# Bulk loads cut into row pieces and issued a few per step from SyncE, with six layer-norm tiles transposed on TensorE

## The chip, the cores and the metric

The kernel runs on one core of a Trainium2 chip. The metric is device time in microseconds (us), as the median of several executions. A kernel's executions mostly lie within 1 to 2% of each other; the comparisons below give a ratio with a 95% interval.

Names used throughout: TensorE (PE, with its weight loads as PEld), VectorE (DVE), ScalarE (ACT), GpSimd (POOL) and SyncE (SP) are the engines; "SPq" and the like are their instruction queues where DMAs are issued. A DMA issued by SyncE goes to the queue q1 of the profile, one by ScalarE to q10, one by GpSimd to q0.

## The reference

Four layers, alternating a linear-attention block A and a sliding-window block B (window 256), forward and then all gradients. B = 1, S = 2048, D = 640, 32 heads of 20, bf16. Both B layers share weights, and so do both A layers.

```python
x = x + A(layernorm(x), A_wqkv, A_wo)     # layer 0: phi(q) (phi(k)^T v) / normalizer, then @ wo
x = x + B(layernorm(x), B_wqkv, B_wo)     # layer 1: softmax over the last 256 keys, then @ wo
x = x + A(layernorm(x), A_wqkv, A_wo)     # layer 2
x = x + B(layernorm(x), B_wqkv, B_wo)     # layer 3
# returned: x and the gradients for A_x, A_wqkv, A_wo, B_wqkv, B_wo, given grad_out
```

## The kernel before

The stages in order of time, as they are named below:

| stage | from ... to | what runs |
|---|---|---|
| start | begin ... first QKV matmul | loads of x and of the weights |
| first | ... first mixing matmul | layer 0: layer norm and QKV of 16 tiles |
| fwd | ... first score matmul of the backward attention | rest of the forward pass |
| gap3 | ... first `acc` product | pipeline of layer 3's attention fills; weights are transposed |
| att3 | ... first dense matmul | backward attention of layer 3, 8 groups of heads x 16 blocks |
| dns3 | ... first weight-gradient matmul | dense backward of layers 3 and 2, up to the start of the next attention |
| att1 | ... last `acc` product | backward attention of layer 1, filled with weight-gradient matmuls of layers 3 and 2 |
| dns1 | ... last dense matmul | dense backward of layers 1 and 0 |
| last | ... end | weight gradients of layers 1 and 0 |

In the attention every unit computes scores, `e` (ACT), `ds` (DVE), and turns `ds` into `dsT`. One half of `dsT` is turned on TensorE, the other half by a DMA transpose that SyncE issues. Five steps later the products `acc` read it. Bulk loads come from three engines:

```python
def dma(self, out, in_, eng=None, piece=None):
    eng = eng or self.nc.scalar                      # ScalarE unless said otherwise
    kw = dict(max_dma_last_dim=piece) if piece else {}
    ...
def tr(self, out, in_):
    self.nc.sync.dma_start_transpose(out=out, in_=in_)      # always SyncE
# ... load_w:
    elif name == "WT":                               # 2400 KB, GpSimd
        self.dma(t, self.WT_d[:, kind], self.nc.gpsimd, piece=D)
# ... flip_w: transposed weights, three buffers in turn
        t = pool.tile([P, n, P], BF, name=f"wt{n}")
        self.tr(t, w[k * P:(k + 1) * P, :])
        if late is not None:
            self.dma(*late, self.nc.gpsimd)          # the store that frees the buffer: GpSimd
# ... seg_first:
    for c in range(0, self.TT, 2):
        self.dma(self.car[:, c:c + 2, :], xv[:, c:c + 2, :])     # x, ScalarE, W after the first
# ... seg_attention_bwd:
    def load(g):                                     # the slabs of a group of heads
        r = slabs[g] = slab_B if g % 2 else self.slab_A
        for i, n in enumerate(("QT", "KT", "VT")):
            if g > 0:
                self.dma(r[n], sv["qkvT"][:, i * G + g, :])      # 512 KB each, ScalarE
        for t in range(0, T, 512 if g == 0 else T):
            ts = slice(t, t + (512 if g == 0 else T))
            self.dma(r["dOT"][:, ts], sv["dOT"][:, g, ts], nc.sync if g == 0 else None)
    def load_rows():                                 # 7.7 MB, GpSimd
        for t in range(0, TT, 4):
            self.dma(qk_r[:, t:t + 4, :], sv["qk"][:, t:t + 4, :], nc.gpsimd)
            self.dma(dO_r[:, t:t + 4, :], sv["dO"][:, t:t + 4, :], nc.gpsimd)
    # ... dscore(u, half, ps):
        if half == 0:
            self.tr(dsT_of[u][:, 0:2 * nkt, :], ds_of[u][:, 0:2 * nkt * P])
# ... wgrad: operands of 2560 and 1280 to 1920 KB, GpSimd
    self.dma(lhs, lhs_d, nc.gpsimd, piece=D)
    ...
    self.dma(r[:, :, 0:w], rhs_d[:, :, c * w:(c + 1) * w], nc.gpsimd)
```

The softmax here doesn't subtract the row's maximum and nothing guards it: scores larger than these inputs give would overflow.

Of the kernel before, what the change touches and what calls it, by code (L numbers as in the profile page):

```python
# [15 lines left out]
P = 128  # L16
# [6 lines left out]
class Kern:  # L23

    def __init__(self, ctx, tc, x0, A_wqkv, A_wo, B_wqkv, B_wo, grad_out, outs):
# [12 lines left out]
        assert D == 640 and T % 512 == 0  # L38
        self.c_att = float(DH) ** -0.5
        self.x0, self.grad_out = x0, grad_out  # L40
        self.out_x4, self.out_gx, self.out_dWA, self.out_dWoA, self.out_dWB, self.out_dWoB = outs
# [77 lines left out]

    def dma(self, out, in_, eng=None, piece=None):  # L120
        eng = eng or self.nc.scalar
        kw = dict(max_dma_last_dim=piece) if piece else {}
        with self.nc.allow_non_contiguous_dma(reason="strided layouts"):
            eng.dma_start(out=out, in_=in_, **kw)

# [13 lines left out]
    def load_w(self, pool, kind, name):  # L139

        D, DT = self.D, self.DT
        if name == "W":
            t = pool.tile([P, DT, self.QT], BF, name=f"W{kind}")
            self.dma(t, self.Wqkv[kind].rearrange("(kt p) n -> p kt n", p=P))
        elif name == "Wo":
            t = pool.tile([P, DT, D], BF, name=f"Wo{kind}")
            self.dma(t, self.Wo[kind].rearrange("(kt p) n -> p kt n", p=P))
        elif name == "WT":
            t = pool.tile([P, self.QTT, D], BF, name=f"WT{kind}")
            self.dma(t, self.WT_d[:, kind], self.nc.gpsimd, piece=D)  # L150
        else:
            t = pool.tile([P, DT, D], BF, name=f"WoT{kind}")
            self.dma(t, self.WoT_d[:, kind], self.nc.gpsimd, piece=D)
        return t

    def permute_w(self):

        w = 4 * DH
        out = self.Wp.rearrange("r (g t c) -> r t g c", t=3, c=w)
        in_ = self.Wqkv[1].rearrange("r (t g c) -> r t g c", t=3, c=w)  # L160
        for t in range(3):
            self.dma(out[:, t], in_[:, t], self.nc.sync)

# [21 lines left out]

    def ln(self, l, tt, pw):
        nc, D = self.nc, self.D
        x = self.car[:, tt, :]
        st = pw.tile([P, 2, nc.vector.BN_STATS_DIM], F32, name="ln_st")
        for c in range(2):  # L190
            nc.vector.bn_stats(st[:, c, :], x[:, c * self.HD:(c + 1) * self.HD])
        mv = pw.tile([P, nc.vector.BN_AGGR_DIM], F32, name="ln_mv")
        nc.vector.bn_aggr(mv, st)
        lv = pw.tile([P, 1], F32, name="ln_lv")
        nc.scalar.activation(lv, mv[:, 1:2], ACT.Ln, bias=self.eps_t, scale=1.0)
        rs = self.rs[l][:, tt:tt + 1]
        nc.scalar.activation(rs, lv, ACT.Exp, scale=-0.5)
        hn = pw.tile([P, D], BF, name="ln_hn")
        nc.vector.tensor_scalar(out=hn, in0=x, scalar1=mv[:, 0:1], scalar2=rs, op0=ALU.subtract, op1=ALU.mult)
        hnT = pw.tile([P, self.DT, P], BF, name="ln_hnT")  # L200
        self.tr(hnT, hn)
        self.dma(self.hn_d[l][:, tt, :], hn)
        return hnT
# [212 lines left out]
    def seg_first(self, acc, pf, pWA, pWB):  # L416

        with ExitStack() as st:
            pw = self.pool(st, "w0w", 3)
            pkv = self.pool(st, "w0kv", 6)  # L420
            pps = self.pool(st, "ps", 8, PSUM)
            xv = self.tm(self.x0)
            for c in range(0, self.TT, 2):
                self.dma(self.car[:, c:c + 2, :], xv[:, c:c + 2, :])
                if c == 0:
                    W = self.load_w(pWA, 0, "W")
            self.Wf = (W, self.load_w(pWB, 0, "Wo"), self.load_w(pf, 1, "Wo"), self.load_w(pWB, 1, "W"))
            tiles = []
            for tt in range(self.TT):
                hnT = self.ln(0, tt, pw)  # L430
                self.drain(self.A_qkv(0, tt, hnT, W, tiles, pw, pkv, pps))
                self.kv_step(tiles, acc, tt, pps)

    def seg_pair(self, l, mbd, acc, on_tail=None):

        nc, TT, H, G = self.nc, self.TT, self.H, self.G
        with ExitStack() as st:
# [78 lines left out]
            for u in range(-AHEAD, n + LAG):  # L516
                if on_tail is not None and u == n - G:
                    on_tail()
                if u + AHEAD < n:
                    evs[u + AHEAD] = self.B_scores(l + 1, *units[u + AHEAD], ring, pe, ps_s)  # L520
# [154 lines left out]
    def load_A(self, l):  # L675
        for i, n in enumerate(("QT", "KT", "VT")):
            self.dma(self.slab_A[n], self.sv[l]["qkvT"][:, i * self.G, :], self.nc.gpsimd)

    def seg_attention_bwd(self, l, fill, pace, side=None):
# [7 lines left out]
        with ExitStack() as st:  # L687
# [8 lines left out]
            def load(g):  # L696
                r = slabs[g] = slab_B if g % 2 else self.slab_A
                for i, n in enumerate(("QT", "KT", "VT")):
                    if g > 0:
                        self.dma(r[n], sv["qkvT"][:, i * G + g, :])  # L700
                for t in range(0, T, 512 if g == 0 else T):
                    ts = slice(t, t + (512 if g == 0 else T))
                    self.dma(r["dOT"][:, ts], sv["dOT"][:, g, ts], nc.sync if g == 0 else None)

# [3 lines left out]
            def load_rows():  # L708
                for t in range(0, TT, 4):
                    self.dma(qk_r[:, t:t + 4, :], sv["qk"][:, t:t + 4, :], nc.gpsimd)  # L710
                    self.dma(dO_r[:, t:t + 4, :], sv["dO"][:, t:t + 4, :], nc.gpsimd)

# [110 lines left out]

            load(0)
            load_rows()
            n = len(units)
            for s in range(n + JL):
                if side is not None:
                    next(side, None)
                if s < n and units[s][1] == 6 and units[s][0] + 1 < G:  # L830
                    load(units[s][0] + 1)
# [39 lines left out]
    def dense_weights(self, l, pool):  # L871
        w = [self.load_w(pool, 1, "WT"), self.load_w(pool, 0, "WoT"), pool.tile([P, 6, self.D], BF, name="mbdT")]
        self.dma(w[2], self.sv[l - 1]["mbdT"], self.nc.gpsimd, piece=self.D)
        return w

    def seg_dense_bwd(self, l, w, mid):

        nc, TT, D, DT, H, HD = self.nc, self.TT, self.D, self.DT, self.H, self.HD
        a = l - 1
        sv = self.sv[a]  # L880
        with ExitStack() as st:
            pb = self.pool(st, "bacc")
# [6 lines left out]
            with ExitStack() as s2:  # L889
# [69 lines left out]
                for s in range(-2, TT + 3):  # L959
                    for f, d in plan:  # L960
                        if 0 <= s + d < TT:
                            f(s + d)
                    if s == 3:
                        WTA = self.load_w(pb, 0, "WT")
                        WoTB = self.load_w(pb, 1, "WoT") if a > 0 else None
# [3 lines left out]
            with ExitStack() as s2:  # L969
# [59 lines left out]
                def flip_dO(t):  # L1029
                    ring, pos = self.dOT_ring[(t // 4) % 2], t % 4  # L1030
                    self.flip(self.do_slabs[t % 3], self.G, ring[:, :, pos * P:(pos + 1) * P], pt, [nc.scalar.copy])
                    if pos == 3:
# [4 lines left out]
                        *tail[2:])  # L1037
                for s in range(-4, TT + 2):
                    for f, d in plan:
                        if 0 <= s + d < TT:  # L1040
# [5 lines left out]

    def wgrad(self, l, pools, last, which=(0, 1), wait=0):

# [5 lines left out]
                (self.o_d[l], self.g_d[l], HD, self.part[kind][1], (self.out_dWoA, self.out_dWoB)[kind], False)]  # L1054
        jobs = [jobs[i] for i in which]
        for lhs_d, rhs_d, w, part, out, perm in jobs:
            lhs = pW.tile([P, TT, D], BF, name="wg_l", bufs=2 if last else 1)
            self.dma(lhs, lhs_d, nc.gpsimd, piece=D)
            n = part.shape[1] // w

            def load(c):
                r = pw.tile([P, TT, wq], BF, name="wg_r")
                self.dma(r[:, :, 0:w], rhs_d[:, :, c * w:(c + 1) * w], nc.gpsimd)
                return r
            rhs = load(0)
            for _ in range(wait):
                yield
            for c in range(n):
                nxt = None
                for m in range(DT):  # L1070
# [5 lines left out]
                    for tt in range(TT):  # L1076
                        nc.tensor.matmul(ps, lhsT=lhs[:, tt, rows], rhs=rhs[:, tt, 0:w],  # L1077
                                         start=(tt == 0), stop=(tt == TT - 1))
                        yield
                    if m == 0 and c + 1 < n:  # L1080
                        nxt = load(c + 1)
                    if last:
# [16 lines left out]
    def run(self):  # L1099
        self.permute_w()  # L1100
        s_att = self.ctx.enter_context(ExitStack())
        with ExitStack() as st:
# [12 lines left out]
            for l in (0, 2):  # L1115
                with ExitStack() as s2:
                    pm = self.pool(s2, "mbd")
                    mbd = self.close_A(l, acc, pm)
                    self.seg_pair(l, mbd, acc, None if l == 0 else tail)
                if l == 0:  # L1120
                    sA.close()
        for l in (3, 1):
            with ExitStack() as s2:
                s_wg, s_ps, w = ExitStack(), ExitStack(), []

                def fill():
                    pools = self.wg_pools(s_wg) + [self.pool(s_ps, "wgp", 1, PSUM)]
                    yield from self.wgrad(3, pools, False, (0, 1), 48)
                    yield from self.wgrad(2, pools, False, (0, 1), 48)
                    s_wg.close()  # L1130
# [15 lines left out]
                else:  # L1146
                    self.seg_attention_bwd(l, it, lambda s: 11.8)
                    self.drain(it)
# [3 lines left out]
                    def mid():  # L1152
# [4 lines left out]
                        def run():  # L1157
                            for k in (1, 0):
                                yield from self.wgrad(k, pools, True, wait=1)
                        last.extend((pools, run()))  # L1160
# [59 lines left out]
```

## Time and profile before

The median was 2788.51 us in the first three runs (2772.23 to 2792.51). The profiled execution has a span of 2800.1 us.

The page of the kernel before. The first line is busy time with its share of the span; then come 40 slices of 70 us each, in tenths: PE busy, the granted TensorE clock, and the busy share of the DMA engines.

```profile
PE 2235.1 (80%) x27724; PEld 1420.6 (51%) x27724; DVE 1360.2 (49%) x2554; ACT 1277.1 (46%) x2171; POOL 1076.5 (38%) x1433
...
PE   3879997489986146998889795897799878969979
...
PEclk9989998698795566787899797898899889979999
DMA  9588984498896998877784775688677669486585
```

TensorE is busy 80% of the time; the other engines are at half or less. It is the engine to keep fed. Weak places of the PE row that the change touches are the beginning and the slices from about 910 to 1120 us, the start of att3. The clock row is weak in the latter too.

The list of waits (engine, line and tile that waited, then what it waited for, total us, times, longest us):

```profile
PE acc L786 <- DMA dsT<-ds: 143.2, 17, 60.1
...
PE d L232 <- DMA ln_hnT<-ln_hn: 59.3, 7, 44.3
...
POOL WoT_d L124 <- DMA qk_r<-qk: 40.3, 2, 36.7
```

The products waited 143.2 us for DMA-transposed tiles, once for 60.1 us. The first QKV matmul waited 44.3 us for its transposed tile.

The DMA queues (packets, MB, share of 16 engines) and some issues (how often, KB each, median us from issue to landing):

```profile
q1 hardware_dynamic: 647888, 198.29, 41.8%
q10 hardware_dynamic: 110624, 142.25, 16.9%
q0 software_dynamic: 35152, 144.56, 16.8%
...
qk_r<-qk POOLq DMA_DIRECT2D x8, 1280.0 KB, 31.6
...
wg_l<-hn POOLq DMA_DIRECT2D x4, 2560.0 KB, 14.9
...
dsT<-ds SPq DMA_TRANSPOSE x256, 4.0
```

The bytes of the bulk loads are in q10 (ScalarE) and q0 (GpSimd); the `dsT` transposes are among the many small packets of q1 (SyncE). A `dsT` tile lands in 4.0 us at the median; the view of that tile gives 26.0 us as the longest.

The 60 us wait can be read from two timelines (start, duration, engine, line, tile; in brackets the idle time before it and what ended it). SyncE around 940 us:

```profile
940.64 57.44 SPq L127 DMA_TRANSPOSE wt<-in_A_wqkv_dram  x2
998.50 5.00 SPq L127 DMA_TRANSPOSE dsT<-ds  x2
```

and GpSimd in the same stretch:

```profile
984.11 0.89 POOL L124 DMA_DIRECT2D WoT_d<-wt  x1 [36.68 <-DMA qk_r<-qk]
```

SyncE stood 57.44 us in front of a weight transpose (`wt`) that had no free buffer. The buffer comes free when GpSimd's store to `WoT_d` or `WT_d` has run. GpSimd had issued the eight row loads from 940.80 to 945.04 us, ahead of that store, and they took 43.0 to 58.1 us to land; the store waited 36.68 us until one of them had landed. The attention's own `dsT` transposes stood behind the weight transpose in SyncE's queue and were issued from 998.50 us on, so TensorE stopped: 60.10 us.

### The profile page before, as it was taken

How to read it: one execution, taken by the hardware profiler on the slowest of the kernel's cores; microseconds unless marked ns; L12 is line 12 of the kernel's file. 1: busy time of each engine (PE TensorE's matmuls, PEld its weight loads, DVE VectorE, ACT ScalarE, POOL GpSimd, SP SyncE). 2: the span in 40 equal slices, each digit the busy share in tenths (PEclk: the TensorE clock that was granted, in tenths of full speed). 3: DMA queues.
4: the chain of work that ended last, by engine and by line, in shares of the span. 5: the costliest groups of instructions: out<-in, count | busy, mean ns of one | idle time of the engine just before them, and what ended most of it. 6: DMA issues, size and time to landing. Idle time of an engine off the chain costs nothing.

```text
span 2800.1 us, 67774 instructions
## 1 busy us (share of the span) xinstructions
PE 2235.1 (80%) x27724; PEld 1420.6 (51%) x27724; DVE 1360.2 (49%) x2554; ACT 1277.1 (46%) x2171; POOL 1076.5 (38%) x1433
## 2 busy tenths in 40 slices
PE   3879997489986146998889795897799878969979
PEld 2545555345453034665556563565566555647445
DVE  4555664354452134676656474454455445626212
ACT  2437777156565035777723342555465442324000
POOL 0035454135455243444456552333333335636010
PEclk9989998698795566787899797898899889979999
DMA  9588984498896998877784775688677669486585
GB/s 239 156 161 180 195 183 128 106 183 184 187 193 170 245 133 173 140 137 129 131 233 133 173 197 224 152 178 184 173 162 167 150 157 219 133 225 181 167 259 174
DMA packets 793976, 489.42 MB, mean 175 GB/s; under 512 B 620384, under 2 KB 754704, under 8 KB 792640
## 3 DMA queue, kind: packets, MB, share of 16 engines
q1 hardware_dynamic: 647888, 198.29, 41.8%
q10 hardware_dynamic: 110624, 142.25, 16.9%
q0 software_dynamic: 35152, 144.56, 16.8%
q8 instruction: 217, 3.56, 0.5%
q14 instruction: 95, 0.78, 0.1%
HBM read 185.27 MB, written 161.19 MB: 124 GB/s over the span
## 4 chain that ended last, share of the span: by engine, by line
PE 32%; DMA 12%; DVE 8%; ACT 4%; issue 4%; SPq 2%; POOL 0%; DVEq 0%; ACTq 0%; POOLq 0%
PE wg L1077 10%; PE acc L786 7%; DMA dsT<-ds 6%; PE sp L727 5%; PE d L601 4%; PE tp L771 3%; PE t L558 2%; DVE dh_u L617 2%; ACT e L741 1%; DVE do_s L583 1%; DVE car L618 1%; SPq L127 1%; DMA vT<-v 1%; DMA wg_pt<-pq1w 1%; ACT dh_s L609 1%
## 5 line engine op out<-in xcount | busy, mean ns | idle before, releaser
L761 DVE SCALAR_TENSOR_TENSOR ds<-sp,e 128x768 bf16<-128x768 f32 (+2 forms) x512 | 462.4, 906 | 475.8 <-PE sp L727 301.5
L741 ACT ACTIVATE e<-sp 128x768 bf16<-128x768 f32 (+2 forms) x512 | 395.3, 775 | 343.4 <-PE sp L727 254.5
L363 ACT ACTIVATE e<-s 128x768 bf16<-128x768 f32 (+2 forms) x512 | 374.3, 774 | 158.8 <-PE s L361 122.9
L1077 PE MATMUL wg<-wg_r,wg_l 128*128 128x320 bf16 (+1 forms) x2240 | 411.7, 326 | 32.5 <-DVE wg_o L1084 24.6
L745 POOL TENSOR_SCALAR_AFFINE_SELECT e<-e 128x512 bf16<-128x512 bf16 x256 | 162.7, 636 | 527.9 <-issue 399.9
L366 POOL TENSOR_SCALAR_AFFINE_SELECT e<-e 128x512 bf16<-128x512 bf16 x256 | 163.8, 640 | 336.9 <-ACT e L363 333.4
L1077 PEld LDWEIGHTS <-wg_l 128*128 128x128 bf16 x2240 | 208.9, 99 | 157.5 <-issue 48.0
L786 PE MATMUL acc<-qk_r,dsT 128*128 128x40 bf16 (+1 forms) x2880 | 129.8, 183 | 146.1 <-DMA dsT<-ds 143.2
L727 PE MATMUL sp<-KT,QT 32*128 32x384 bf16 (+2 forms) x1024 | 186.8, 361 | 59.0 <-ACT e L741 53.8
L232 PE MATMUL d<-W,ln_hnT 128*128 128x320 bf16 x960 | 158.6, 319 | 64.4 <-DMA ln_hnT<-ln_hn 59.3
L786 PEld LDWEIGHTS <-dsT 128*128 128x128 bf16 x2880 | 102.6, 99 | 204.7 <-DMA dsT<-ds 148.0
L727 PE MATMUL sp<-VT,dOT 32*128 32x384 bf16 (+2 forms) x1024 | 187.3, 357 | 21.5 <-DVE ds L761 13.2
L320 PE MATMUL d<-W,ln_hnT 128*128 128x480 bf16 x640 | 185.8, 414 | 12.6 <-DVE o_b L389 8.5
L361 PE MATMUL s<-ring 32*128 32x128 bf16 x2880 | 163.1, 233 | 27.4 <-ACT e L363 25.6
L217 PE MATMUL d<-Wo,oT 128*128 128x320 bf16 x640 | 133.8, 335 | 55.3 <-DMA oT<-o_t 49.4
L601 PE MATMUL d<-WT,dqkvT 128*128 128x320 bf16 x960 | 147.4, 309 | 21.9 <-issue 11.2
L232 PEld LDWEIGHTS <-ln_hnT 128*128 128x128 bf16 x960 | 93.7, 103 | 111.4 <-DMA ln_hnT<-ln_hn 60.5
L771 PE MATMUL tp<-ident,ds 128*128 128x128 bf16 x1440 | 144.4, 243 | 7.1 <-DVE ds L761 6.5
L809 ACT CAST dqkv_o<-acc 128x240 bf16<-128x240 f32 x256 | 92.2, 360 | 125.8 <-PE acc L786 121.7
L361 PEld LDWEIGHTS <-ring 32*128 32x128 bf16 x2880 | 81.5, 97 | 128.4 <-issue 120.5
L369 POOL TENSOR_SCALAR_AFFINE_SELECT e<-e 128x512 bf16<-128x512 bf16 x224 | 144.5, 645 | 0.0
L749 POOL TENSOR_SCALAR_AFFINE_SELECT e<-e 128x512 bf16<-128x512 bf16 x224 | 142.4, 636 | 0.0
(159 smaller groups left out, 3970.8 us busy)
## 6 DMA issues: line engine op xcount, KB each, us to landing
qkvT<-ring ACTq DMA_DIRECT2D x32, 768.0 KB, 5.8
dqkv<-dqkv_o POOLq DMA_DIRECT2D x32, 480.0 KB, 4.5
wg_r<-dqkv POOLq DMA_DIRECT2D x12, 1280.0 KB, 9.2
wg_r<-dqkv POOLq DMA_DIRECT2D x8, 1920.0 KB, 10.5
hn<-ln_hn ACTq DMA_DIRECT2D x64, 160.0 KB, 2.7
qk<-qk_flat ACTq DMA_DIRECT2D x64, 160.0 KB, 3.8
qk_r<-qk POOLq DMA_DIRECT2D x8, 1280.0 KB, 31.6
hn_ld<-hn SPq DMA_DIRECT2D x64, 160.0 KB, 3.3
```

Source lines behind the costliest of these rows:

```text
L232: nc.tensor.matmul(ps, lhsT=hnT[:, k, :], rhs=W[:, k, ci * HD:(ci + 1) * HD], start=(k == 0), stop=(k == self.DT - 1))
L320: nc.tensor.matmul(ps, lhsT=hnT[:, k, :], rhs=W[:, k, ci * 480:(ci + 1) * 480], start=(k == 0), stop=(k == self.DT - 1))
L361: nc.tensor.matmul(ps[:, j, i * P:(i + 1) * P], lhsT=ring[r0:r0 + HP, G + g, kt * P:(kt + 1) * P], rhs=ring[r0:r0 + HP, g, qs], start=True ...
L363: nc.scalar.activation(ev[:, 2 * half:2 * half + 2], ps[:, :, 0:nkt * P].rearrange("p h (i q) -> p h i q", q=P), ACT.Exp, scale=self.c_att)
L366: nc.gpsimd.affine_select(out=ev[:, :, nkt - 1, :], in_=ev[:, :, nkt - 1, :], compare_op=ALU.is_ge, fill=0.0, base=0, pattern=[[0, 4], [1, ...
L601: self.nc.tensor.matmul(ps[:, c, 0:self.HD], lhsT=w, rhs=WT[:, k, c * self.HD:(c + 1) * self.HD], start=(k == 0), stop=(k == len(lhs) - 1))
L727: nc.tensor.matmul(ps[:, j, 0:nkt * P], lhsT=slabs[g][ta][r0:r0 + HP, b * P:(b + 1) * P], rhs=slabs[g][tb][r0:r0 + HP, k0 * P:(k0 + nkt) * P],
L741: nc.scalar.activation(ev[:, 2 * half:2 * half + 2], ps[:, :, 0:nkt * P].rearrange("p h (i k) -> p h i k", k=P), ACT.Exp, scale=c_att)
L761: nc.vector.scalar_tensor_tensor(out=dv[:, hs], in0=ps[:, :, 0:nkt * P].rearrange("p h (i k) -> p h i k", k=P), scalar=c_att, in1=ev[:, hs ...
L771: nc.tensor.transpose(tp[:, i * P:(i + 1) * P], ds_of[u][:, (nb + i) * P:(nb + i + 1) * P], self.ident)
L786: nc.tensor.matmul(acc[:, hh * DH:hh * DH + w], lhsT=lhsT, rhs=rhs(rname, g, t, hh, w), start=(i == 0), stop=(i == len(s) - 1), skip_group ...
L1077: nc.tensor.matmul(ps, lhsT=lhs[:, tt, rows], rhs=rhs[:, tt, 0:w], start=(tt == 0), stop=(tt == TT - 1))
```

## The change

The intent: cut every bulk load into pieces of 1 to 2.5 KB per partition (128 to 320 KB in all), and issue them from SyncE, a few with every step, so that never more than a few hundred KB lie ahead of a transpose. The first six layer-norm tiles are transposed on TensorE, since SyncE and the DMA engines are busy with x and W at that time. No bytes are added or removed. The core of the diff:

```diff
+    def later(self, pairs):
+        self.queue.extend(pairs)
+    def drip(self, n):
+        while self.queue and n > 0:
+            self.dma(*self.queue.pop(0), self.nc.sync)
+            n -= 1
 # load_w
-            self.dma(t, self.WT_d[:, kind], self.nc.gpsimd, piece=D)
+            pairs = [(t[:, k, :], self.WT_d[:, kind, k, :]) for k in range(self.QTT)]
 # ... (the same for W, Wo, WoT, mbdT, and for the permuted copy of W in permute_w)
+        self.later(pairs)
 # seg_first
-            pps = self.pool(st, "ps", 8, PSUM)
+            pps = self.pool(st, "ps", 7, PSUM)
+            pt = self.pool(st, "pt", 1, PSUM)
 # ... (x and W queued in pieces, x's first two tiles first)
-                hnT = self.ln(0, tt, pw)
+                hnT = self.ln(0, tt, pw, pt if tt < 6 else None)     # TensorE transposes
+                self.drip(2)
 # seg_attention_bwd
-                for t in range(0, T, 512 if g == 0 else T):
-                    self.dma(r["dOT"][:, ts], sv["dOT"][:, g, ts], nc.sync if g == 0 else None)
+                for t in range(0, T, 512):
+                    ts = slice(t, t + 512)
                     if g > 0:
-                        self.dma(r[n], sv["qkvT"][:, i * G + g, :])
+                        self.later([(r[n][:, ts], sv["qkvT"][:, i * G + g, ts]) for i, n in ...])
+                    self.later([(r["dOT"][:, ts], sv["dOT"][:, g, ts])])
-                for t in range(0, TT, 4):
-                    self.dma(qk_r[:, t:t + 4, :], sv["qk"][:, t:t + 4, :], nc.gpsimd)
-                    self.dma(dO_r[:, t:t + 4, :], sv["dO"][:, t:t + 4, :], nc.gpsimd)
+                for t in range(TT):
+                    self.later([(qk_r[:, t, :], sv["qk"][:, t, :]), (dO_r[:, t, :], sv["dO"][:, t, :])])
             for s in range(n + JL):
+                self.drip(3 if s < TT else 2)
-                if s < n and units[s][1] == 6 and units[s][0] + 1 < G:
+                if s < n and units[s][1] == 3 and units[s][0] + 1 < G:
                     load(units[s][0] + 1)
 # wgrad: per-tile pieces from nc.sync with yields between, instead of whole loads from nc.gpsimd
 # run: permute_w is called after the first segment instead of first of all
```

Against the schedule, SyncE's plain DMAs go from 359 to 1178, ScalarE's from 530 to 462 and GpSimd's from 247 to 180. (The limit `max_dma_last_dim`, `piece` in the code, that some of GpSimd's loads had is gone.)

## The prediction

> **What bounds the kernel now.** The timed median is 2788.5 us. The page's busy shares are PE 80%, DVE 49%, ACT 46%, POOL 38%: TensorE is the engine to keep fed. Where PE stands still (windows view): 0-44 us, no matmul; 907-1010 (start of the first backward attention), 10 of 103 us busy with the DMA share at 1.13; 1010-1398, 331 of 388; 1727-1756 (start of the second backward attention), 1.7 of 29; 1756-2305, 475 of 549; 2590-2800, 182 of 210. The list of waits says on what: 44.3 us on the first transposed layer-norm tile; `acc` on `dsT<-ds` 88 us in the first attention (one wait of 60.1) and 55 us in the second (eight, up to 14.9). A `dsT` transpose lands in 4.0 us at the median but in 26.0 at worst. The slow ones lie right behind bulk loads: eight row loads of 640 and 1280 KB (median 31.6 us to land), `wg_l` of 2560 KB (14.9), WT of 2400 KB (13.9), four slab loads of 512 KB per head group. [...]POOL's and ACT's loads delay SyncE's transposes.
>
> **What changes.** Bytes stay the same. The schedule of instructions shows SyncE's plain DMAs going from 359 to 1178, ACT's from 530 to 462, POOL's from 247 to 180; SyncE's transposes 639 to 633. A plain issue costs SyncE 0.32 us, about 0.26 ms more of issue over the run; a `dsT` issue costs 1.21 us. Per attention unit (2.9 us in the first, 4.2 in the second) SyncE gets 1.2 us of transpose and one to three pieces of 0.33 us: it fits, with little room while the weights are flipped.
>
> **On the critical path, my estimate by stage:**
> - Start: ACT is stuck 28 us issuing `car` and TensorE starts at 44. With W and x in pieces, the weight permutation moved behind them, and transposes on PE, it starts near 14: -30. In SyncE's order 14 permutation pieces (about 1.3 us each, from 18.8 us for the three now) stand before the seventh tile's transpose: +8.
> - 907-1010: rows come as needed, and the weight flips no longer wait behind 7.7 MB: -65.
> - 1010-1398: WT, slab bursts: -25.
> - 1727-1756: -15.
> - 1756-2305: waits on `dsT` from 55 us to about 10: -45.
> - 2305-2590: waits of 20.6, 16.0 and 15.4 us in the chain behind WT and `wg_l`: -20.
> - 2590-2800: -8.
> - Given back: transposes in SyncE's in-order queue behind pieces that wait for a buffer or for an earlier DMA: +20.
>
> Sum -180: **2610 us**, 8 in 10 between 2530 and 2700. Faster by over 2%: 0.90; within 2%: 0.08; slower: 0.02.
>
> **What would show it.** First matmul before 20 us; PE busy over 50% in the 100 us after the forward; the longest `dsT` landing under about 12 us, and PE's wait for `dsT` under 50 us in all; the second attention about 500 us long.
>
> **What would make it wrong.** SyncE becomes the bottleneck: transposes late because pieces ahead of them wait, so the `dsT` waits become many and short instead of few and long. DMA work itself limiting the first attention (share 0.81 there now), so that moving loads only spreads the stall. TensorE's granted clock (0.76 there) dropping as it gets denser. A gap at about 40-60 us while the seventh tile waits for the permutation.

That loads of other engines delay SyncE's transposes is read from the profile before: of its 256 `dsT` transposes, 131 were in flight together with a bulk load of GpSimd or ScalarE and landed in 5.1 us at the median and 26.0 at most (47 took over 6 us); the other 125 landed in 3.3 and 6.9 (4 over 6).

## The result

The changed kernel takes 2618.97 us (median of 4, 2613.21 to 2636.11) against 2780.37 us for the kernel before (median of 4): ratio 0.943, 95% interval 0.9363 to 0.9497.

The page of the changed kernel, the same four rows as before:

```profile
PE 2226.9 (85%) x27754; PEld 1415.2 (54%) x27754; DVE 1360.1 (52%) x2554; ACT 1279.7 (49%) x2177; POOL 1009.4 (39%) x1366
...
PE   5879998759897656799989898799999987989999
...
PEclk8889998778878555689999899699889898989999
DMA  9589877289979699988897574989888859669687
```

Busy time of PE is the same within 0.4% (2226.9 against 2235.1 us); 177 of the 185 us came out of its idle time. The list of waits:

```profile
PE acc L805 <- DMA dsT<-ds: 45.0, 26, 6.3
...
PE d L246 <- ACT ln_hnT L579: 16.6, 6, 7.7
```

The products' wait on DMA transposes fell from 143.2 to 45.0 us, the longest from 60.1 to 6.3. By stage (the same list for a window of time): in gap3 from 60.1 to 1.7 us, in att1 from 55.0 to 7.3, but in att3 it rose from 28.1 to 35.8. The QKV matmuls of the first six tiles now wait for ScalarE, which copies the tiles out of PSUM. The DMA queues and the same issues:

```profile
q1 hardware_dynamic: 788928, 331.93, 60.8%
q10 hardware_dynamic: 97760, 103.71, 13.0%
q0 software_dynamic: 13856, 48.51, 6.4%
...
qk_r<-qk SPq DMA_DIRECT2D x32, 320.0 KB, 4.9
...
wg_l<-hn SPq DMA_DIRECT2D x64, 160.0 KB, 3.6
...
dsT<-ds SPq DMA_TRANSPOSE x256, 3.7
```

134 MB have moved into q1. A row piece lands in 4.9 us instead of 31.6, and the longest `dsT` landing is 8.6 us instead of 26.0.

The spans of the stages, in us, each marked by the first or last matmul that the stage table names:

| kernel | start | first | fwd | gap3 | att3 | dns3 | att1 | dns1 | last | span |
|---|---|---|---|---|---|---|---|---|---|---|
| before | 44.3 | 81.3 | 791.4 | 92.9 | 389.7 | 359.5 | 544.3 | 288.0 | 208.7 | 2800.1 |
| changed | 8.8 | 108.6 | 797.1 | 31.8 | 375.4 | 329.5 | 501.7 | 275.6 | 186.4 | 2614.9 |
| difference | -35.5 | +27.3 | +5.7 | -61.1 | -14.3 | -30.0 | -42.6 | -12.4 | -22.3 | -185.2 |

The fwd stage varies by some 30 us between kernels in which nothing of it was touched (778.7 to 809.8 in the runs below), so its +5.7 means nothing.

### The profile page after: what moved, and what is told of

It is laid out like the page before. It is cut to its first block, busy times and chain, and to the rows that moved or that the text cites. A ratio compares the mean times of both kernels' runs of the same rounds, so it can differ in the third digit from the quotient of the medians.

```text
span 2614.9 us, 68629 instructions
## 1 busy us (share of the span) xinstructions
PE 2226.9 (85%) x27754; PEld 1415.2 (54%) x27754; DVE 1360.1 (52%) x2554; ACT 1279.7 (49%) x2177; POOL 1009.4 (39%) x1366
## 5 line engine op out<-in xcount | busy, mean ns | idle before, releaser
L246 PE MATMUL d<-W,ln_hnT 128*128 128x320 bf16 x960 | 169.3, 332 | 47.2 <-DMA ln_hnT<-ln_hn 23.2
L233 DVE TENSOR_TENSOR car<-d,car 128x320 bf16<-128x320 f32 x128 | 62.3, 486 | 145.2 <-PE d L231 144.7
```

The source lines that it names most:

```text
L246: nc.tensor.matmul(ps, lhsT=hnT[:, k, :], rhs=W[:, k, ci * HD:(ci + 1) * HD], start=(k == 0), stop=(k == self.DT - 1))
```

## The experiments

Twelve kernels were run, and all gave correct results. Their stages, in us (one profiled execution each), and the timed medians:

| run | start | first | fwd | gap3 | att3 | dns3 | att1 | dns1 | last | span | median | ratio to before, 95% |
|---|---|---|---|---|---|---|---|---|---|---|---|---|
| e1 start only | 8.8 | 108.6 | 790.1 | 84.8 | 380.2 | 359.5 | 543.5 | 285.8 | 210.7 | 2772.0 | 2777.16 | 0.9951 (0.9902-1.0) |
| e2 old start | 44.9 | 81.7 | 782.3 | 36.2 | 378.6 | 327.4 | 500.5 | 273.8 | 187.0 | 2612.4 | 2634.26 | 0.9423 (0.9359-0.9486) |
| e3 unpaced | 8.8 | 107.2 | 781.9 | 51.3 | 361.7 | 354.4 | 491.0 | 270.0 | 207.3 | 2633.6 | 2650.98 | 0.9485 (0.9427-0.9542) |
| e4 whole loads | 8.8 | 106.1 | 783.8 | 43.9 | 352.3 | 356.1 | 476.9 | 270.4 | 209.5 | 2607.8 | 2614.48 | 0.9362 (0.9305-0.942) |
| e5 before, SyncE | 43.8 | 81.6 | 796.3 | 50.9 | 349.4 | 341.0 | 484.9 | 271.1 | 213.8 | 2632.8 | 2627.33 | 0.9407 (0.9334-0.9481) |
| e6 pieces, GpSimd | 8.8 | 106.4 | 779.6 | 35.8 | 368.4 | 350.2 | 520.4 | 319.3 | 184.0 | 2672.9 | 2690.55 | 0.9675 (0.9576-0.9775) |
| e7 whole, GpSimd | 8.8 | 107.4 | 796.5 | 40.3 | 377.8 | 387.0 | 530.5 | 305.0 | 211.6 | 2764.9 | 2770.06 | 0.9928 (0.9854-1.0002) |
| e8 16 tiles on PE | 8.9 | 123.5 | 784.7 | 32.7 | 369.2 | 329.6 | 503.9 | 278.4 | 185.3 | 2616.2 | 2630.04 | 0.9421 (0.9346-0.9497) |
| e9 before, ScalarE | 44.8 | 84.2 | 800.7 | 87.6 | 385.0 | 381.9 | 535.1 | 324.4 | 193.3 | 2837.0 | 2808.81 | 1.0062 (0.995-1.0174) |
| e10 mix | 8.9 | 108.1 | 795.2 | 32.4 | 357.1 | 333.5 | 482.4 | 277.4 | 184.3 | 2579.3 | 2582.85 | 0.9252 (0.9169-0.9335) |
| e11 rows, SyncE | 43.8 | 81.2 | 809.8 | 52.9 | 409.9 | 343.4 | 548.9 | 289.5 | 209.6 | 2789.0 | 2780.85 | 0.9961 (0.9881-1.0041) |
| e12 slabs, SyncE | 43.7 | 81.3 | 778.7 | 60.9 | 357.5 | 358.7 | 532.3 | 291.1 | 207.3 | 2711.5 | 2722.26 | 0.9737 (0.9693-0.9782) |

Two theories stood at the outset. Theory A is the prediction's: what hurts is the number of bytes issued at one time ahead of a transpose, so the pieces and the pacing win. Theory B, the rival: the issuing engine wins, whatever the size. (From e5 on, Theory C is B, put as a matter of the queue. Theory D is one thing in e6 and e7, when loads are asked for, and another in e12.)

### e1: the new start alone

```diff
 # before, with seg_first, load_w of W and Wo, permute_w and ln of the changed kernel
+            self.later(x[:2]); W = self.load_w(pWA, 0, "W"); self.later(x[2:]); self.drip(len(self.queue))
+                hnT = self.ln(0, tt, pw, pt if tt < 6 else None)
```

> The kernel before with only the new start (x and W in pieces on SyncE, permutation later, six layer-norm tiles transposed on TensorE); every later load as before. Theory A: the 35 us by which the first matmul comes earlier are nearly all handed back inside the first stage, so the whole run gains 5 to 12 us (ratio about 0.996 to 0.998) and the first mixing matmul (on pqT) starts near 117 us instead of 126. Rival B: the start is worth what TensorE gains at its beginning, about 30 us (ratio about 0.989).

Measured: 2777.16 us, ratio 0.9951 with an interval that ends at 1.0. TensorE starts 35.5 us earlier, and the following stage is 27.3 us longer, so layer 0's first mixing matmul comes 8 us earlier (117.4 us against 125.6). The start is worth about 0.5%.

### e2: everything but the new start

```diff
 # changed, with seg_first and the first call of permute_w of before
-                hnT = self.ln(0, tt, pw, pt if tt < 6 else None)
+                hnT = self.ln(0, tt, pw)
```

> The changed kernel with the start of the kernel before. Theory A: it keeps about 150 of the 161 us (ratio about 0.947), first matmul near 44 us, the later stages as in the changed kernel. Rival B: it keeps only about 130 us (ratio about 0.954).

Measured: 2634.26 us, ratio 0.9423. The gain of the change lies in the backward half. The two runs agree: the start is worth 0.5% or less.

### e3: the same pieces from SyncE, without pacing

```diff
     def later(self, pairs):
-        self.queue.extend(pairs)
+        for p in pairs:
+            self.dma(*p, self.nc.sync)
 # and in wgrad all pieces of an operand at once
```

> The changed kernel with the same pieces on the same engine, but all of a load's pieces issued at once, where the load is asked for. Theory A (bytes ahead of a transpose at one time, so pacing, is what counts): the stalls on dsT return, first accumulation of the first attention near 980 us or later instead of 946, the longest dsT landing over 15 us, total 2680 to 2740 us. Rival B (it is enough that the loads left ACT's and POOL's queues, or that pieces are small): within 15 us of the changed kernel, about 2620 to 2635.

Measured: 2650.98 us, outside both ranges: below that of A, and 32 us above the changed kernel where B allowed 15. So far as A speaks of pacing it is refuted: without it most of the gain stays. What pacing wins lies outside the attentions (last 207.3 against 186.4, dns3 354.4 against 329.5, gap3 51.3 against 31.8); in the attentions the burst is even faster (361.7 and 491.0 against 375.4 and 501.7).

### e4: whole loads from SyncE, paced, in the backward half

```diff
-            pairs = [(t[:, k, :], self.WT_d[:, kind, k, :]) for k in range(self.QTT)]
+            pairs = [(t, self.WT_d[:, kind])]
-                for t in range(0, T, 512):
-                    ts = slice(t, t + 512)
+                st = 512 if g == 0 else T
+                for t in range(0, T, st):
+                    ts = slice(t, t + st)
 # and so for WoT, mbdT, the rows (as before: four tiles at a time) and the operands of wgrad
```

> The changed kernel with SyncE issuing and the pacing kept, but from the first backward attention on each load whole as in the kernel before (512 KB slabs, 640 and 1280 KB rows, weights 0.8 to 2.4 MB, gradient operands 1.3 to 2.5 MB); the start as changed. Theory A: a whole load is a burst by itself, so dsT waits of 10 to 20 us return in both attentions, total 2680 to 2750 us. Rival B (only the engine that issues matters): about 2620 to 2640.

Measured: 2614.48 us, ratio 0.9362, as fast as with pieces. Theory A falls. Pieces cost time in the attentions (375.4 and 501.7 us with them, 352.3 and 476.9 without) and win it in gap3, in dns3 and in the last stage.

### e5: the kernel before with one thing changed, the issuing engine

```diff
-            self.dma(t, self.WT_d[:, kind], self.nc.gpsimd, piece=D)
+            self.dma(t, self.WT_d[:, kind], self.nc.sync)
-                        self.dma(r[n], sv["qkvT"][:, i * G + g, :])
+                        self.dma(r[n], sv["qkvT"][:, i * G + g, :], nc.sync)
-                    self.dma(qk_r[:, t:t + 4, :], sv["qk"][:, t:t + 4, :], nc.gpsimd)
+                    self.dma(qk_r[:, t:t + 4, :], sv["qk"][:, t:t + 4, :], nc.sync)
 # and so for all other bulk loads of the backward half; sizes, places and the start as before
```

> The kernel before with one thing changed: the loads of the backward half (slabs, rows, transposed weights, mbdT, gradient operands) are issued by SyncE instead of GpSimd and ScalarE; whole, at the old places, the old start. Theory C (the loads' queue counts[...]): most of the gain, 2640 to 2680 us, and dsT waits of TensorE about 60 us in all. Theory A (pieces and pacing count): little gain, 2740 to 2790 us.

Measured: 2627.33 us against 2797.54, ratio 0.9407. This one edit gives as much as the whole change. Theory B holds: no pieces, no pacing, no new start. (As the diff shows, the edit also drops the limit `piece=D`. It does not explain the gain: e9 drops it too and gains nothing, and e4 and e7, both without it, are nearly as far apart, by 156 us, as e5 and e9, by 181.)

### e6 and e7: the paced pieces, and the paced whole loads, issued by GpSimd

```diff
     def drip(self, n):
-            self.dma(*self.queue.pop(0), self.nc.sync)
+            self.dma(*self.queue.pop(0), self.dripper)       # SyncE in the forward half, GpSimd after it
 # e6 on the changed kernel, e7 on e4; the operands of wgrad likewise
```

> The changed kernel, its pieces and its pacing kept, but from the backward half on the pieces are issued by GpSimd. Theory C: the pieces in GpSimd's queue stretch the dsT transposes again, but each only for a short time: 2650 to 2710 us, median dsT landing above 4 us. Theory D (what counts is when loads are asked for, so that none piles up): within 15 us of the changed kernel, 2610 to 2640 us.

> The changed kernel's pacing with whole loads (as in the coarse run, which took 2614 us from SyncE), issued by GpSimd. Theory C: dsT waits of 10 to 20 us return, 2680 to 2760 us. Theory D: 2610 to 2650 us, as from SyncE.

Measured: 2690.55 and 2770.06 us. From GpSimd the size does matter: pieces are 80 us better than whole loads. But the best that GpSimd gives is still some 70 us short of SyncE. In att3 of e6 the products waited 4.3 us on `dsT`, against 35.8 in the changed kernel, and the stage was only 7.0 us shorter; in att1 they waited 10.6 us against 7.3, and it was 18.7 us longer. The dense stages lose 64 us together; there GpSimd also computes, and issues the loads between its computations, which may be the reason but was not tested. So the wait on `dsT` that the prediction was built on does not set the time alone. Something else had to be found.

### e8: all 16 layer-norm tiles of the start on TensorE

```diff
-                hnT = self.ln(0, tt, pw, pt if tt < 6 else None)
+                hnT = self.ln(0, tt, pw, pt if tt < 16 else None)
```

> The changed kernel with all 16 tiles of the first layer norm transposed on TensorE instead of six. If the first stage gives its early start back because the seventh tile's DMA transpose stands behind 14 permutation pieces in SyncE's queue (issued from 40 to 59 us): the first mixing matmul starts at 100 to 108 us instead of 117, total about 10 us less. Rival (the stage is bound by the arrival of x and W, and by ScalarE's order): it starts at 113 to 118 us, total unchanged.

Measured: 2630.04 us, and the first mixing matmul comes at 132.4 us instead of 117.4. The idea that the seventh tile's place in SyncE's queue causes the give-back of the start fell as the main cause: taking the tile out of the queue made it worse, and TensorE's wait for ScalarE's copies rose from 16.6 to 31.1 us. The seventh tile does stand there, though. SyncE's timeline of the changed kernel:

```profile
40.27 18.58 SPq L124 DMA_DIRECT2D Wp<-in_B_wqkv_dram  x14
59.05 3.61 SPq L136 DMA_TRANSPOSE ln_hnT<-ln_hn  x2
```

The 14 pieces of the weight permutation take 18.58 us of SyncE, about 1.3 us each, and the seventh tile's transpose follows at 59.05; TensorE waited 3.53 us for it. ScalarE's copies, with 16.6 us, are the larger part of the 27 us. The remaining 7 us are not assigned; that x now arrives behind W may be part of them and was not tested.

### e9: the kernel before, with GpSimd's loads issued by ScalarE

```diff
-            self.dma(t, self.WT_d[:, kind], self.nc.gpsimd, piece=D)
+            self.dma(t, self.WT_d[:, kind], self.nc.scalar)
 # and so for every bulk load of the backward half; same places, same sizes as e5
```

> The kernel before; its bulk loads of the backward half that GpSimd issued are issued by ScalarE instead (ScalarE already issued the slab loads), whole, at their old places; the old start. It differs from e5 only in the issuing engine. Theory C1 (the transposes of dsT and of the weights sit in SyncE's queue, and a load in ANY other queue [...]stretches them; only in SyncE's own queue does it not): as slow as before, 2760 to 2830 us, PE's wait on dsT in the products at 100 us or more. Theory C2 (the harm is GpSimd's: its loads stand in its in-order instruction stream in front of the weight stores that SyncE's transposes wait for[...]): most of e5's gain, 2620 to 2690 us, PE's wait on dsT at 60 us or less, and SyncE's 57 us block at 940 us gone. A middle result, 2690 to 2760, would say that both count; ScalarE waiting at its own loads would show as idle time of ScalarE before them.

Measured: 2808.81 us, ratio 1.0062: no gain. e9 and e5 differ in nothing but the issuing engine, and e5 is 180 us faster. So the harm is not GpSimd's alone. But one part of the expectation failed: PE's wait on `dsT` was nearly as low as in e5. In the list of waits, first e9, then e5:

```profile
PE acc L786 <- DMA dsT<-ds: 39.6, 13, 6.7
```

```profile
PE acc L786 <- DMA dsT<-ds: 35.2, 11, 13.5
```

Half of the fall from 143.2 us is only a change of name: in gap3 the kernel before has 60.1 us of this wait; e9 has 4.5, but its gap3 is 87.6 us long all the same, because ScalarE's first exponential, which has ScalarE's own row loads in front of it, stood 87.9 us (the list puts the wait down to a weight transpose, `wt`). In the two attentions proper the wait was 83.1 us before, 35.1 in e9 and 21.6 in e5. These differ little, yet the attentions of e9 and e5 differ by 86 us. Where is that time? The windows view over the two attentions (us of the stretch; busy us of each engine with instructions in brackets; granted clock, DMA share, GB/s). First before, then e9, e5 and the changed kernel:

```profile
1010.00:1400.00 390.00, 331.40 (x6030) 222.79 (x6031) 251.67 (x313) 267.64 (x438) 173.88 (x268) 0.76 0.81 145
1759.00:2303.00 544.00, 473.02 (x7304) 309.31 (x7305) 272.95 (x350) 293.92 (x488) 183.32 (x273) 0.90 0.74 164
```

```profile
1017.00:1402.00 385.00, 337.52 (x6044) 223.51 (x6044) 255.71 (x317) 270.29 (x442) 161.40 (x257) 0.77 0.80 138
1784.00:2319.00 535.00, 485.81 (x7316) 314.06 (x7317) 274.01 (x351) 292.87 (x491) 159.03 (x253) 0.93 0.76 171
```

```profile
973.00:1322.00 349.00, 311.32 (x5996) 214.25 (x5993) 245.83 (x308) 263.18 (x435) 166.66 (x258) 0.81 0.90 170
1663.00:2148.00 485.00, 453.72 (x7279) 302.88 (x7280) 265.18 (x340) 289.48 (x482) 154.81 (x245) 0.96 0.83 189
```

```profile
946.00:1322.00 376.00, 316.01 (x6028) 216.35 (x6029) 250.20 (x313) 264.43 (x437) 168.73 (x262) 0.80 0.91 176
1651.00:2153.00 502.00, 473.07 (x7314) 308.06 (x7314) 271.92 (x348) 293.67 (x489) 158.20 (x251) 0.93 0.84 187
```

In e9 the same matmuls keep TensorE busy 58 us longer than in e5 (337.52 + 485.81 against 311.32 + 453.72), at a granted clock of 0.77 and 0.93 instead of 0.81 and 0.96. Only 28 of the 86 us are idle time. The busy time hides a loss: a matmul at half clock counts as busy, and takes longer. In the kernel before, TensorE is busy 23.01 of the 24 us from 1212 to 1236, at a clock of 0.50, with 336 matmul records; from 1236 to 1260, at 1.00, it is busy 22.67 us with 484. A score matmul of 384 columns takes 498 ns at the mean in the first stretch (`KT`, `QT`) and 331 in the second. (Two cautions: the profiled execution of e9 is 30 us above its median, and up to that much of the difference may belong to this one execution; and e5's view holds 85 matmul records fewer, since some are missing from a trace.)

A fall of the clock can be watched at one load of a group's slabs. ScalarE's issues in e9:

```profile
1290.30 0.33 ACTq L124 DMA_DIRECT2D QT<-qkvT  x1
...
1292.72 0.33 ACTq L124 DMA_DIRECT2D KT<-qkvT  x1
...
1303.60 0.33 ACTq L124 DMA_DIRECT2D VT<-qkvT  x1
```

TensorE in the same place:

```profile
1302.05 0.56 PE L786 MATMUL acc<-qk_r,dsT 128*128 128x40 bf16 x12 [3.61 <-DMA dsT<-ds]
```

and the windows view there, in slices of 3 us (the columns as above; look at PE busy and at the granted clock):

```profile
1295.00:1298.00 3.00, 3.00 (x75) 2.26 (x71) 1.46 (x3) 2.49 (x5) 0.64 (x1) 1.00 1.13 124
1298.00:1301.00 3.00, 0.44 (x4) 0.10 (x3) 0.89 (x2) 1.55 (x3) 1.22 (x2) 0.82 1.46 95
1301.00:1304.00 3.00, 1.95 (x35) 1.32 (x36) 0.69 (x1) 0.36 (x1) 0.00 (x0) 0.50 1.01 101
...
1310.00:1313.00 3.00, 2.82 (x48) 1.87 (x48) 1.92 (x2) 2.22 (x4) 1.12 (x2) 0.50 1.00 218
...
1316.00:1319.00 3.00, 3.00 (x50) 2.03 (x47) 2.17 (x3) 2.63 (x4) 1.17 (x3) 0.50 0.34 66
1319.00:1322.00 3.00, 2.81 (x61) 1.95 (x59) 2.16 (x3) 2.62 (x5) 1.15 (x3) 0.76 0.35 66
1322.00:1325.00 3.00, 2.88 (x76) 2.09 (x73) 2.63 (x4) 2.34 (x5) 1.72 (x4) 1.00 0.77 51
```

QT and KT are issued at 1290 and 1293 us; ScalarE does not stand still at them, so it is not its queue that is blocked here. The `dsT` transposes issued from 1290 to 1311 us land in up to 10.5 us (median 5.8), and TensorE stands still for 3.61 us. Then the clock is 0.50 for about 20 us, although TensorE is busy nearly all of that time. The stretch at half clock costs an estimated 7 us on top of the stall of 3.6 us: a third of 20 us, since 50 matmul records run from 1316 to 1319 us at 0.50 and 75 from 1295 to 1298 at 1.00. The next fall comes 48 us later, with the next group's slabs. The same place in e5, with the four slab loads issued by SyncE between 1188.7 and 1196.2 us, each with a transpose between:

```profile
1195.00:1198.00 3.00, 2.65 (x56) 1.80 (x52) 1.61 (x4) 2.77 (x7) 1.19 (x2) 1.00 1.10 371
1198.00:1201.00 3.00, 2.78 (x38) 1.63 (x36) 2.26 (x3) 2.97 (x5) 1.81 (x4) 0.78 1.56 246
1201.00:1204.00 3.00, 3.00 (x52) 1.97 (x49) 2.62 (x4) 1.98 (x3) 1.59 (x3) 0.50 0.90 229
1204.00:1207.00 3.00, 2.91 (x62) 2.15 (x62) 1.91 (x3) 2.68 (x4) 1.23 (x2) 0.59 0.70 136
1207.00:1210.00 3.00, 2.99 (x64) 2.04 (x63) 2.86 (x5) 2.56 (x5) 1.97 (x4) 1.00 0.37 67
```

The transposes land in 5.6 us at most (median 5.0), no stall is seen, and the clock is at half for some 7 us. The last two columns differ as well: from 1298 to 1304 us the DMA engines of e9 are as busy as those of e5 from 1195 to 1204, but move 95 and 101 GB/s instead of 229 to 371.

This is one place, and it stands for the first attention only. Of the transposes issued there between 2 us before and 8 us after a slab load, 21 of 64 took over 6 us in e9 and 8 of 50 in e5; in the second attention 8 of 38 in e9 and 11 of 26 in e5, the other way round. Late transposes beside slab loads do not explain why e9's second attention is longer.

A share of the difference between e9 and e5 as large as that of the attentions lies in the dense stages: dns3 and dns1 together are 94.2 us longer in e9. Two waits of TensorE make 64.5 us of it, and in e5 it has neither:

```profile
PE d L601 <- DMA dqkvT<-dqkv: 64.5, 2, 35.3
```

At both places a `dqkvT` transpose of SyncE was in flight together with the whole load of WT (2400 KB), issued less than 1.1 us apart. In e9 ScalarE issues WT: at the first place the transpose lands after 36.0 us and WT after 37.3, at the second after 43.0 and 45.1. In e5 SyncE issues both: WT lands after 11.5 and 9.5 us, the transpose behind it after 14.1 and 13.7. From GpSimd (e7, also whole) WT takes 15.8 and 11.2 us, and the transpose issued within 1.6 us before it 13.9 and 8.9. The DMA view of e9 from 1403 to 1437 us shows the engines busy throughout and 98 GB/s moved; that of e5 from 1341 to 1356 us shows 294 GB/s. So at these two places a transpose from SyncE and a whole load from ScalarE slowed each other down, and the DMA engines moved a third of the bytes in the same time; the load from GpSimd had no such effect. Without these 64.5 us e9 would be an estimated 2744 us (2808.81 less 64.5): that it equals the kernel before comes from losses that are partly others. In e5, e7 and e9 WT, 19,200 bytes per partition, goes without the limit `piece=D`; in the kernel before, with it, its packets are of 4,320 and 4,480 bytes. Whether ScalarE's queue with the limit would do the same was not run.

At the slab load of e9 shown above a stall of 3.61 us and a fall of the clock from 1.00 to 0.50 come together. That the stall sets off the fall is not shown: three falls without such a stall are named under what stays open. The stretches at half clock, counted in slices of 1 us, mostly last 3, 7, 10, 14, 17, 20 or 24 us (12 of the 18 in the two attentions of the kernel before). TensorE need not be idle in them: in the kernel before the clock stayed at half from 1212 to 1236 us with TensorE busy for 23.0 of the 24 us.

To compare kernels, both attentions were cut into slices of 2 us, and the slices with a granted clock below 0.75 added up:

| kernel | att3 + att1, us | half clock in att3 | half clock in att1 | together |
|---|---|---|---|---|
| before | 934.0 | 188 | 110 | 298 |
| e9 before, ScalarE | 920.1 | 182 | 70 | 252 |
| e12 slabs, SyncE | 889.8 | 140 | 98 | 238 |
| e6 pieces, GpSimd | 888.8 | 174 | 64 | 238 |
| changed | 877.1 | 152 | 68 | 220 |
| e10 mix | 839.5 | 124 | 34 | 158 |
| e5 before, SyncE | 834.3 | 130 | 42 | 172 |
| e4 whole loads | 829.2 | 118 | 38 | 156 |

The order of times is nearly the order of time at half clock. But a slice in which TensorE stands still counts here too, and idle time alone gives nearly the same order: 130 us before, then 97, 102, 84, 89, 70, 69 and 73 from e9 to e4. The rest is busy time: 804 us before, then 824, 788, 805, 789, 770, 765 and 756. So the clock is a part of the loss and not shown to be the whole of it. e9 has 80 us more at half clock than e5; with a third of it lost, as in the records above (50 against 75), that is an estimate of 27 of the 58 us of longer busy time. The ends of matmuls are modelled in such a profile, and the other 31 us were not assigned.

### e10: whole loads while the attention's steps run, pieces elsewhere

```diff
 # changed; pieces kept for the rows, the first slabs, the dense weights and the last weight gradients
-                for t in range(0, T, 512):
-                    ts = slice(t, t + 512)
+                st = 512 if g == 0 else T
+                for t in range(0, T, st):
+                    ts = slice(t, t + st)
-                    self.dma(lhs[:, tt, :], lhs_d[:, tt, :], nc.sync)      # filling wgrad only
-                    for _ in range(3): yield
+                self.dma(lhs, lhs_d, nc.sync)
+                for _ in range(48): yield
-                return r, [(r[:, t:t + 2, 0:w], rhs_d[...]) for t in range(0, TT, 2)]
+                k = 2 if last else TT
+                return r, [(r[:, t:t + k, 0:w], rhs_d[...]) for t in range(0, TT, k)]
```

> The changed kernel with whole loads where the steps of the attention run (the slabs of the next group of heads in four loads of 512 KB, the operands of the two filling weight gradients whole), and pieces kept at the start of the attention, for the dense weights and in the last weight gradients. If the stage table of e4 and of the changed kernel adds up (pieces cost some 23 us in each attention and win 23 us in the last stage and 26 us in and before the first dense stage): 2560 to 2590 us, with the attentions at about 352 and 477 us and the last stage at 186 us. Rival (what the pieces win and cost is one sum of time that only moves from stage to stage): 2605 to 2630 us.

Measured: 2582.85 us, ratio 0.9252. The stage table added up: the attentions take 357.1 and 482.4 us, the last stage 184.3. This beats the changed kernel by 36 us and e4 by 32 (the intervals of the last two ratios still overlap a little, 0.9335 against 0.9305), and shows that the pieces do cost time in the attentions: 37.6 us in both together, with 62 us less at half clock.

### e11: only the rows to SyncE

```diff
-                    self.dma(qk_r[:, t:t + 4, :], sv["qk"][:, t:t + 4, :], nc.gpsimd)
-                    self.dma(dO_r[:, t:t + 4, :], sv["dO"][:, t:t + 4, :], nc.gpsimd)
+                    self.dma(qk_r[:, t:t + 4, :], sv["qk"][:, t:t + 4, :], nc.sync)
+                    self.dma(dO_r[:, t:t + 4, :], sv["dO"][:, t:t + 4, :], nc.sync)
```

> The kernel before; only the row loads qk_r and dO_r of each attention (8 loads) go from GpSimd to SyncE, everything else as before. e5 moved all loads and won 170 us. If the row loads in front of GpSimd's weight stores make the stall before the first attention, the stage before it falls from 93 to about 45 to 55 us, and the run takes 2725 to 2755 us; the loads of filling operands and slabs then carry the rest of the 170 us. Rival (loads inside the attention carry nearly all, the row loads only move the wait): 2770 to 2800 us.

Measured: 2780.85 us, ratio 0.9961. Half of the expectation held: gap3 fell from 92.9 to 52.9 us, so the row loads in front of GpSimd's stores do make much of that gap. But att3 grew by 20.2 us, and the time of the run is the same. The rival held: taken alone, this moves most of the wait.

### e12: only the slabs to SyncE

```diff
-                        self.dma(r[n], sv["qkvT"][:, i * G + g, :])
+                        self.dma(r[n], sv["qkvT"][:, i * G + g, :], nc.sync)
-                    self.dma(r["dOT"][:, ts], sv["dOT"][:, g, ts], nc.sync if g == 0 else None)
+                    self.dma(r["dOT"][:, ts], sv["dOT"][:, g, ts], nc.sync)
```

> The kernel before; only the slab loads of the later groups of heads (QT, KT, VT, dOT of 512 KB each, four per group, 56 in both attentions) go from ScalarE to SyncE, whole, at their old places; rows, weights and weight-gradient operands stay with GpSimd. New theory D (a load in another queue holds up the few transposes of dsT that are in flight for some 4 us once per group of heads; TensorE stands still for 3 to 4 us, and its granted clock then stays at half for about 17 us, which costs more than the stall; in SyncE's own queue the transposes come through): the long stretch at half clock that recurs with every group shrinks from some 20 to under 10 us; half-clock time falls from 188 to about 140 us in the first attention, and from 110 to 90 us or less in the second; the run takes 2690 to 2735 us, the first attention 340 to 360 us. Rival (the slab loads alone don't matter, only all loads together): 2770 us or more.

Measured: 2722.26 us, ratio 0.9737. The 56 slab loads alone give 76.6 us. In att3 the time at half clock fell from 188 to 140 us as expected, the stretches after the first 130 us last 6 to 10 us, and the stage takes 357.5 us. Of the 32 us that this stage gains, 21.5 are idle time and 10.7 busy time. In att1 it fell only to 98 us, more than expected: there the operands of the filling weight gradients still come from GpSimd, and the three long stretches (22 to 24 us) remain that e5 has cut to 6 to 10. gap3 also fell by 32 us, which the theory had not said; in this run SyncE stood 30 us instead of 57 at the same weight transpose.

## Why the prediction was right or wrong

The time was right (2610 predicted, 2618.97 measured), and so was every mark that the prediction set: first matmul at 8.8 us, PE busy 62% in the 100 us after the forward pass, longest `dsT` landing 8.6 us, 45.0 us of waiting for `dsT`, second attention 501.7 us. TensorE's wait on late transposes was rightly seen as what there was to gain in gap3 and att1. The remedy to which the prediction put the gain down was for the most part not what worked. The number came out all the same because the bundle held the right remedy, the issuing engine, beside the one it counted on, and no mark told the two apart: that is luck.

- **The step that failed** is the cost of a load by its size: "The slow ones lie right behind bulk loads", "rows come as needed", "WT, slab bursts: -25". It took pieces and pacing to be the remedy. e4 gave the same time with whole loads, e3 most of it without pacing, and e5 all of it with nothing but another issuing engine. In the two attentions the pieces cost 37.6 us (changed against e10).
- **What was read from the profile** was taken too far. The prediction read rightly that loads of other queues delay SyncE's transposes (5.1 against 3.3 us at the median, 26.0 against 6.9 at most, as told beside it), but sought the remedy in spreading the bytes and had no term for the issuer. e9 and e5 differ only in the issuer, by some 180 us. Two things that depend on it can be seen. One is what stands behind the loads in the issuing engine's own order of instructions: in gap3 the store that frees a buffer stood behind row loads in GpSimd's queue and waited 36.68 us, and in e9 ScalarE's exponentials waited up to 87.9 us for a weight transpose (`wt`), against 37.6 before. The other is how transposes fare beside a load: beside ScalarE's load of WT they took 36.0 and 43.0 us to land, behind the same load in their own queue 14.1 and 13.7; at the slab load shown above up to 10.5 us against 5.6. It is not a rule for every load: over all of its `dsT` transposes e5 is no faster than e9 (medians 4.3 and 3.8 us, longest 19.6 and 12.9).
- **The waits were summed without the clock.** The prediction took the waits on `dsT` off the time ("from 55 us to about 10: -45"). In att1 that was sound: the waits fell by 47.7 us, the stage by 42.6, and the busy time stayed (473.02 and 473.07 us). In att3 it was not: the waits rose by 7.7 us, and what the stage gained is busy time (331.40 to 316.01 us). In e9 the waits in the attentions fell by 48.0 us and the two stages by only 13.9. The stall of 3.6 us shown above is followed by some 20 us at half clock, which shows as busy time. The last paragraph of the prediction saw a low clock in att3 but feared it would fall as TensorE got denser; it rose, from 0.76 to 0.80.
- **Start: -30, then +8.** Measured -35.5 and then +27.3. The step mis-sized is the second: the permutation pieces cost 3.5 us of waiting; ScalarE's copies, which the prediction had left out, cost 16.6, and some 7 us are not assigned. e1 puts the whole start at 0.5%.
- **907-1010: -65.** Measured -61.1, and e11 confirms that the row loads in GpSimd's queue are behind much of it.
- **1010-1398: -25.** Measured -14.3; with whole slabs it would have been -32.6 (e10). The pieces gave the difference back.
- **1727-1756: -15 and 2305-2590: -20.** The stages dns3 and dns1 gained 30.0 and 12.4 us, together 42 against 35.
- **1756-2305: -45.** Measured -42.6, with the wait on `dsT` at 7.3 us where about 10 was forecast. e5 gets there with whole loads (9.9 us, stage 59.4 us shorter than before), and so does e10 (7.0 us, -61.9).
- **2590-2800: -8.** Measured -22.3. Here the pieces and the pacing do win: e3, e4 and e5, which lack one or both, stay at 207 to 214 us. TensorE's idle time behind `wg_o` in that stage, which waits for loads of partial sums (VectorE waited 94.0 us for them before and 38.3 after), fell from 24.6 to 1.2 us. But e9, whole and unpaced from ScalarE, takes 193.3 us there, so pieces are not the only way; that was not followed up.
- **Given back: +20.** The right size for what pieces cost in each attention (23.1 and 24.8 us against e4), but counted once. The way foretold, transposes behind pieces in SyncE's queue, fits att3, where the products waited 35.8 us on `dsT` against 17.4 in e10; in att1 they waited as long in both (7.3 and 7.0), and the cause there is open. Two misses, this one and the start, were made good by the last and the dense stages.

What stays open: why a transpose and a whole load slow each other so when SyncE and ScalarE issue them. In e9 packets of WT and of SyncE's small transfers start together in 32 of the 34 us from 1403 to 1437, and in e5 not a single small packet starts from 1344 to 1349 us while WT's run. That does not say why fewer bytes are moved in all (98 GB/s against 294), nor why GpSimd's load did no such harm. Whether transposes and loads could as well share ScalarE's queue was not tried. Nor does a stall precede every fall of the clock: in the 8 us ahead of the falls at 1212 us in the kernel before, at 1201 us in e9 and at 1200 us in e5, no slice of 1 us is idle by more than 0.4. That a fall costs busy time is shown (in the slices of e9 above, 75 matmul records run in 3 us at full clock and 50 at half); what sets off each of them, and why some last 7 us and others 24, is not.

## What to carry to other kernels

When a change bundles several parts, run each alone before believing the reason: here one word per load, the engine that issues it, gave as much as the whole rewrite. Try bulk loads in the queue of the small transfers that must not be late, out of the queues of engines that compute: here that alone gave 170 us. Then test pieces stage by stage: here they cost 37.6 us in the attentions and won 23 in the last stage. Read the granted clock beside the waits: at the place shown here a stall of 3.6 us was followed by 20 us at half clock, an estimated 7 us lost. And set marks that tell the believed cause from the other parts of the bundle; here all marks came true although the remedy believed in was mostly not needed.
